# A decay attention with a softplus feed-forward on one core: the first score tile with 128 stationary columns, the magnitudes' sums listed later, the decay's parts on GpSimd, a shorter warm-up

## The chip, the cores and the metric

The kernel runs on one core of one Trainium2 chip. The metric is the device time of one execution in microseconds (us), the median of three runs. The engines are called as in the profile: PE is TensorE (PEld its weight loads), DVE VectorE, ACT ScalarE, POOL GpSimd, and SP issues nearly all DMAs (its queue is SPq in the rows).

## The reference

Eight batches of eight heads with 576 tokens and 64 features a head go through causal attention with a decay; its output, as 4608 rows of 512, goes through a feed-forward of 2048 with a softplus.

```python
scores = scale * np.matmul(q, k.transpose(0, 1, 3, 2))
cum = np.cumsum(np.log(np.clip(f, 0.0001, 1.0)), axis=-1)
decay = cum[:, :, :, None] - cum[:, :, None, :]
scores = np.where(causal, -1000000000.0, scores + decay)
attn = np.exp(scores - np.max(scores, axis=-1, keepdims=True))
attn = attn / (np.sum(attn, axis=-1, keepdims=True) + 1e-09)
x = np.matmul(attn, v)              # then (4608, 512)
h = x @ w_in
out = (np.maximum(h, 0.0) + np.log1p(np.exp(-np.abs(h)))) @ w_out
```

## The kernel before

The work is written as a list of small operations, and a planner in the kernel (`Plan`) turns the list into the five engines' programs. Each operation has an engine or a choice of engines, a cost, the operations that it needs and the buffers that it takes. The planner takes the operation that can start first by its costs, the one listed earlier when two are equal, appends it to its engine's program, and goes on. The result is a fixed order for each engine; on the chip an engine runs its program in that order and waits where an input is not there yet. A cost that differs from the chip's durations therefore makes no error in the result, only a wait.

**Jobs.** Attention is cut into jobs. Jobs 0 to 13 do batch 0 in float32, jobs 14 to 21 do batch 1 (their scores in float32, called mixed), and from job 22 on each job is one head of batches 2 to 7, 48 jobs, with float16 parts: q and k are each split into a high and a low float16 plane in a tile `T`. A job has five tiles of query rows: tile 0 has 64 rows, tiles 1 to 4 have 128. `stat_tile` lists the scores of a tile as two products into one PSUM bank (L1231 and L1233), then DVE's row minimum (L1238) and ACT's exponential (L1273), which frees the bank. Four banks serve the scores and other attention products. In the profile `s<-T` is a score product; the form `128*64 128x64 f16` means 128 contraction rows, 64 stationary columns and 64 moving columns. After the scores come the transposes or transposing DMAs, and the products with v (L1477, L1561).

**Feed-forward.** Blocks of 128 to 512 tokens run between the attention's operations: `h` products (L1676 in float32 for the first blocks, L1695 in float16), the softplus on ACT and DVE, and `acc` products (L1797, L1778).

**Magnitudes' sums.** Before a batch's float16 parts can be made, `size` finds how large v, q and k are. For each pair of heads of the batch eight jobs ahead it loads v (tile `vp`, L822) and q and k (tile `stage`, L836, two DMAs of 288 KB), and ACT sums the magnitudes (L829 and L840). `spread_tops` turns the sums into scales. A load's cost to the planner is an estimate from its size; the sum that needs it is placed where that estimate ends.

**Decay's parts.** `decay_parts` writes the cumulated decay of all 64 heads as three float16 rows (`eighth`, on ACT or DVE), with two subtractions on DVE between them (`remain`, L572 and L574), and stores them with two DMAs (L577). They are listed with job 13 and are needed from job 22 on.

**Start.** `warm` (L1969) puts three float32 products of 448 columns at the head of PE's program. While the planner's PE idles for over 0.5 us before the first `acc` product, `fill_gap` adds products without use (`fill`, L1984).

Of the kernel before, what the change touches and what calls it, by code (L numbers as in the profile page):

```python
# [30 lines left out]
SPARE_BIAS = 0.5  # L31
# [1 line left out]
WINDOW = 700  # L33
RATE = 262
PLAIN = 0
WARM = 3
CROSS = 2.2
FFN_RANK = 0
SHORT = 512
LARGE = 16.7  # L40
DELAY = 2
VALUES = 2.3

W_FROM, W_EACH = 0, 3
# [16 lines left out]
class Plan:  # L61
# [32 lines left out]
    def give(self, tag, ops, back=None):  # L94

        left = [len(ops), 0.0, back]
        for op in ops:
            self.gives.setdefault(op, []).append((tag, left))
# [105 lines left out]
def on_act(n, more=0.0, psum=False):  # L204
    return On("ACT", (0.067 if psum else 0.095) + n / 1200 + more)


def on_dve(n, fast=False, port=False, bias=0.0):
    return On("DVE", 0.071 + n / (1920 if fast else 960), bias, fast or port)
# [22 lines left out]
NO_ENGINE = On("", 0.0)  # L232
# [41 lines left out]
def tile_decay_attention_softplus_ffn(  # L274
# [18 lines left out]
    B, D, H, _, S = qkT.shape  # L293
    NT, DM = out.shape
    DFF = w_in.shape[1]
    P = 128
# [23 lines left out]
    add, give = plan.add, plan.give  # L320

    def add_dma(emit, kb, n=1, eng="SP", **more):
        return add(on_dma(kb, n, eng), emit, lag=dma_lag(kb, n, eng), **more)
# [20 lines left out]
    def back(box, key):  # L344
        return lambda: box[key, "back"]()
# [19 lines left out]
    MW = 448  # L365
# [133 lines left out]
    def decay():  # L499
        box = {}  # L500

        def load(e):
            box["f"] = buf("raw", [P, S], "fs")[0:BH]
            e.dma_start(out=box["f"], in_=f)

        def clip(e):
            e.tensor_scalar(box["f"], box["f"], 1e-4, 1.0, ALU.max, ALU.min)

        def log(e):
            e.activation(box["f"], box["f"], AF.Ln)  # L510

        def begin(e):
            cum["x"] = buf("x32", [P, NCC, S], "cum")[0:BH]
            cum[0] = cum["x"][:, 1, :]

        def eights(e, t, value):
            e.memset(cum["x"][:, t, :], value)

        def scan(e, a, z):
            c, x = cum[0], box["f"][:, a:z]  # L520
            e.tensor_tensor_scan(c[:, a:z], x, x, c[:, a - 1 : a] if a else 0.0, ALU.add, ALU.min)

        def split(e):
            ch, cl = box["hl"] = [buf("raw", [P, S], f"ch{x}", F32R)[0:BH] for x in "hl"]
            e.tensor_copy(ch, cum[0])
            e.tensor_sub(cl, cum[0], ch.bitcast(F32))

        def twice(ap):
            return bass.AP(ap.tensor, ap.offset, [ap.ap[0], [0, 2], ap.ap[1]])

        def store(e, r):
            x = aug_d[:, r, 0, :]
            to = bass.AP(x.tensor, x.offset, [x.ap[0], [5 * S, 2], x.ap[1]])
            e.dma_start(out=to, in_=twice(box["hl"][r].bitcast(F32)))

        def constant(e, r):
            e.dma_start(out=aug_d[:, 2 * r : 2 * r + 2, 1 - r, :], in_=twice(cum["x"][:, 2 - 2 * r, :]))

        f_ = add(NO_ENGINE, begin, takes=("x32",), lag=0.0)
        set_ = [  # L540
            add(on_fill(S), lambda e, x=x: eights(e, *x), after=[f_]) for x in ((2, 8.0), (0, -8.0))
        ]
        o = add_dma(load, BH * S / 256, takes=("raw",))
        o = add(on_dve(S, True), clip, after=[o])
        l = add(on_act(S), log, after=[o])
        decay_ready["eights"] = set_
        c = l
        for x, a, z in (("quad", 0, P), ("first", P, 2 * P), ("sums", 2 * P, S)):
            on = On("DVE", 0.11 + (z - a) / 480)
            c = decay_ready[x] = add(on, lambda e, a=a, z=z: scan(e, a, z), after=[c])  # L550
        give("raw", [c])
        def rest(after):
            s = add(On("DVE", 1.05, 0.0, True), split, after=[c, *after], takes=("raw", "raw"), loose=True)
            w = [add_dma(lambda e, r=r: store(e, r), BH * S / 128, after=[s] + first_rows) for r in range(2)]
            k = [add_dma(lambda e, r=r: constant(e, r), BH * S / 128, after=set_ + first_rows) for r in range(2)]
            for x in w:
                give("raw", [x])
            decay_ready["rows"] = add(NO_ENGINE, mark, after=w + k, lag=0.0)
            cum_used.extend([s] + k)

        def parts():
            def eighth(e, i):
                if i == 0:
                    box["rest"] = buf("raw", [P, S], "rest")[0:BH]
                    times(e, rows16[0:BH, 0], cum[0], 8.0)
                else:
                    copy(e, rows16[0:BH, i], box["rest"])

            def remain(e, i):
                x, of = box["rest"], rows16[0:BH, i]  # L570
                if i == 0:
                    e.scalar_tensor_tensor(x, cum[0], 8.0, of, ALU.mult, ALU.subtract)  # L572
                else:
                    e.tensor_sub(x, x, of)  # L574

            def store_parts(e, t):
                e.dma_start(out=aug16[:, SR - SR * t : 2 * SR - SR * t, t], in_=rows16[0:BH])  # L577

            o = [c]
            for i in range(SR):  # L580
                on = [on_act(S), on_dve(S, True, bias=SPARE_BIAS)]
                o = [add(on, lambda e, i=i: eighth(e, i), after=o, takes=() if i else ("raw",))]
                if i < SR - 1:
                    o = [add(subs(S), lambda e, i=i: remain(e, i), after=o)]
                if i == 0:
                    cum_used.extend(o)
            give("raw", o)
            decay_ready["parts"] = [add_dma(lambda e, t=t: store_parts(e, t), 216, after=o) for t in range(2)]

        return rest, parts  # L590
# [225 lines left out]
    def size(b, h):  # L816

        box = {}

        def load(e):  # L820
            box["v"] = buf("vpk", [P, 2, NCH * D], f"vp{b}_{h}")
            e.dma_start(  # L822
                out=box["v"].rearrange("p h (c d) -> p h c d", c=NCH),
                in_=vR[b, h - 1 : h + 1].rearrange("h p c d -> p h c d"),
            )

        def norm(e):
            x, at = box["v"].rearrange("p h c -> p (h c)"), h // 2
            e.activation(x, x, AF.Abs, scale=2.0**-16, accum_out=sizes[b % 2][:, at : at + 1])  # L829

        qk = stage[:, NBL * P : NBL * P + 2 * S]

        def load_qk(e):
            for i in range(2):
                to = qk[64 * i : 64 * i + 64].rearrange("p (h s) -> p h s", h=2)
                e.dma_start(out=to, in_=qkT[b, :, h - 1 : h + 1, 1 - i])  # L836

        def norm_qk(e):
            at = H // 2 + h // 2
            e.activation(qk, qk, AF.Abs, scale=2.0**-16, accum_out=sizes[b % 2][:, at : at + 1])  # L840

        if h % 2 == 0:
            return
        ld = add_dma(load, 320, takes=("vpk",))
        r = [add(on_act(2 * NCH * D, 0.19), norm, after=[ld] + size_read.get(b - 2, []))]
        give("vpk", r)
        if b > 1:
            ld = add_dma(load_qk, 576, 2, takes=("qkp",))
            r.append(add(on_act(2 * S, 0.19), norm_qk, after=[ld] + size_read.get(b - 2, [])))
            give("qkp", r[1:])  # L850
        size_ops.setdefault(b, []).extend(r)
        if h == H - 1:
            (spread_sizes if b < 2 else spread_tops)(b)
# [150 lines left out]
    def attention(job):  # L1004
# [200 lines left out]
        def stat_tile(ti):  # L1205
# [12 lines left out]
            for i, (a, z, acc) in enumerate(pieces):  # L1218
# [3 lines left out]
                def scores(e, box=box, a=a, z=z):  # L1222
                    o = keep_bank(box, "bank", "att", f"s{n}_{ti}_{a}")[:, 0 : z - a]
                    box["o"] = o[0:n_q]
                    if plain:
                        e.matmul(  # L1226
                            o, part32(0, q0, q0 + P), part32(1, a, z), start=True, stop=not quad,
                        )
                        return
                    o = box["o"]  # L1230
                    e.matmul(o, qA[:, q0:end], kA[:, a:z], start=True, stop=False)  # L1231
                    r = ST if mixed_ else S16
                    e.matmul(o, qB[0:r, q0:end], kB[0:r, a:z], start=False, stop=True)  # L1233

                def row_min(e, box=box, w=z - a, i=i, final=final):
                    right = MW - P + n_q if final else w
# [730 lines left out]
    warming = {}  # L1967

    def warm(e):  # L1969

        o = keep_bank(warming, "o", "h", "warm")
        for _ in range(WARM):
            e.matmul(o[:, 0:MW], cmask[:, 0:P], cmask, start=True, stop=True)

    give("h", [add(On("PE", 1.3 * WARM), warm, takes=("h",), after=mask_set)], back(warming, "o"))

    filling = []

# [9 lines left out]
    for n in range(len(jobs) + 1):  # L1988
# [26 lines left out]
            units.append(cur["fin"])  # L2015
        if n == nplain:
            plan.slack = SLACK
        if n == nstart - 1:
            decay_parts()
        if n == nfirst:  # L2020
            decay_rest(wrote[0][0][2:])
# [74 lines left out]
```

## Time and profile before

| | |
|---|---|
| median of three runs | 1037.95 us (1036.82 to 1038.4) |
| the profiled execution: its own time | 1036.13 us |
| its span, first to last instruction | 1034.4 us |
| PE busy | 1015.8 us of the span |
| DVE and ACT busy | 816.3 and 812.7 us |
| POOL busy | 87.6 us |
| mean granted TensorE clock | 0.997 |

The span and the profiled execution's own time differ by 1.7 us, which lies before the first and behind the last instruction. That execution is 1.8 us below the median of the three runs. Matmuls are pipelined, so PE's busy time says that it had something in flight, not that it ran at its peak; how far apart two products start tells more.

### The profile page before, as it was taken

What the parts mean: (1) busy time and instruction counts of PE and PEld (TensorE: products, weight loads), DVE (VectorE), ACT (ScalarE), POOL (GpSimd) and SP (SyncE); (2) the same over time, 40 slices, a digit from 0 to 9 for tenths busy, and PEclk for the clock granted to TensorE, in tenths of its full rate; (3) what the DMA queues carried; (4) which work ended last, traced back from release to release, by engine and by line L of the source; (5) the groups of instructions that cost most, each with busy time, mean ns of one, the idle gap of its engine ahead of it and who ended that gap; (6) DMA issues with size and microseconds to landing.
All of it is one profiled execution on the core that took longest, in us unless ns stands there. A gap on an engine that the chain in (4) does not pass through costs nothing.

```text
span 1034.4 us, 19420 instructions
## 1 busy us (share of the span) xinstructions
PE 1015.8 (98%) x6545; PEld 596.8 (58%) x6545; DVE 816.3 (79%) x2287; ACT 812.7 (79%) x1948; POOL 87.6 (8%) x182
## 2 busy tenths in 40 slices
PE   8999999989999999999999999999999999999998
PEld 6767777757655544456655544456655544456554
DVE  7789999879978997798879988898778988652332
ACT  7789899879879888888878997788768887654554
POOL 3233100100010000100010000100010000000000
PEclk9999999989999999999999999999999999999999
DMA  9968765656876586696666677556635564410000
GB/s 238 277 216 267 184 174 128 158 147 153 199 175 157 147 191 162 138 200 170 160 155 155 171 194 154 126 127 158 151 93 120 128 154 106 76 47 24 22 1 30
DMA packets 250931, 150.83 MB, mean 146 GB/s; under 512 B 194496, under 2 KB 225728, under 8 KB 250832
## 3 DMA queue, kind: packets, MB, share of 16 engines
q1 hardware_dynamic: 250664, 149.45, 58.4%
q8 instruction: 51, 0.84, 0.3%
q14 instruction: 48, 0.39, 0.1%
q10 hardware_dynamic: 168, 0.15, 0.0%
HBM read 72.00 MB, written 11.39 MB: 81 GB/s over the span
## 4 chain that ended last, share of the span: by engine, by line
PE 81%; ACT 6%; DVE 6%; DMA 4%; issue 2%; SPq 1%; POOL 0%; DVEq 0%; ACTq 0%; POOLq 0%
PE h L1695 30%; PE acc L1778 28%; PE o L1561 4%; PE s L1231 3%; PE s L1233 3%; PE acc L1797 3%; PE h L1676 2%; DMA stage<-in_qkT 2%; PE s L1226 2%; ACT p L1273 2%; PE o L1477 1%; PE b L1421 1%; DVE s L1238 1%; ACT stage L840 1%; DMA stage<-cross 1%
## 5 line engine op out<-in xcount | busy, mean ns | idle before, releaser
L1778 PE MATMUL acc<-wo,gh 128*128 128x512 f16 x1632 | 381.8, 379 | 0.3 <-ACT gh L264 0.2
L1695 PE MATMUL h<-xh,wi 128*128 128x256 f16 (+2 forms) x1536 | 372.0, 318 | 1.9 <-ACT p L1273 0.9
L1695 PEld LDWEIGHTS <-wi 128*128 128x128 f16 x2304 | 221.7, 98 | 133.1 <-issue 6.3
L1778 PEld LDWEIGHTS <-gh 128*128 128x128 f16 x1632 | 157.2, 98 | 169.1 <-ACT gh L264 0.7
L1695 PE MATMUL h<-xl,wi 128*128 128x256 f16 (+2 forms) x768 | 231.9, 318 | 0.7 <-DVE xl L1650 0.7
L1273 ACT ACTIVATE p<-s,negm 128x288 f32<-128x288 f32 (+7 forms) x384 | 183.0, 480 | 39.9 <-DVE negm L1238 34.8
L1741 DVE SCALAR_TENSOR_TENSOR e<-e,x 128x512 f32<-128x512 f32 (+1 forms) x152 | 95.3, 627 | 82.1 <-ACT e L1729 81.7
L1726 ACT ACTIVATE e<-h,h_down 128x512 f32<-128x512 f32 (+1 forms) x152 | 96.8, 637 | 74.8 <-PE h L1695 74.5
L1238 DVE CUSTOM_DVE_ANT_0 s<-s,cmask,s_down 64x64 f32<-64x64 f32 (+4 forms) x240 | 114.8, 490 | 32.0 <-PE s L1233 28.2
L1752 DVE SCALAR_TENSOR_TENSOR gh<-e,g_up,gh 128x512 f16<-128x512 f32 (+1 forms) x152 | 104.5, 688 | 24.4 <-ACT gh L264 23.9
L264 ACT ACTIVATE gh<-e,g_up 128x512 f16<-128x512 f32 (+1 forms) x116 | 77.9, 672 | 37.2 <-DVE e L1741 36.0
L1231 PE MATMUL s<-T 128*64 128x64 f16 (+1 forms) x336 | 96.6, 299 | 5.0 <-ACT p L1273 4.0
L1733 ACT ACTIVATE x<-h,h_down 128x512 f32<-128x512 f32 (+1 forms) x152 | 96.7, 636 | 0.1
L1729 ACT ACTIVATE e<-e 128x512 f32<-128x512 f32 (+1 forms) x160 | 93.7, 586 | 0.0
L1233 PE MATMUL s<-T 70*64 70x64 f16 (+1 forms) x336 | 92.5, 282 | 0.1
L1273 ACT ACTIVATION_READ_ACCUMULATOR p<-s,negm 128x1 f32 (+1 forms) x384 | 75.9, 198 | 0.0
L1345 DVE SCALAR_TENSOR_TENSOR stage<-p,rsum,stage 64x64 f16<-64x64 f32 (+3 forms) x144 | 70.7, 517 | 0.1
L1345 DVE SCALAR_TENSOR_TENSOR cross<-p,rsum,cross 64x64 f16<-64x64 f32 (+3 forms) x144 | 70.4, 518 | 0.0
L1289 POOL TENSOR_TENSOR lsum<-lsum,part 128x5 f32<-128x5 f32 x48 | 16.0, 333 | 575.3 <-ACT p L1273 575.3
L1561 PE MATMUL o<-stage,v 128*64 128x64 f16 (+4 forms) x408 | 53.2, 284 | 0.0
L1561 PE MATMUL o<-cross,v 128*64 128x64 f16 (+4 forms) x408 | 53.2, 284 | 0.0
L1238 DVE DVE_READ_ACCUMULATOR2_ANT negm<- 128x1 f32 (+1 forms) x384 | 52.9, 138 | 0.0
(183 smaller groups left out, 1289.0 us busy)
## 6 DMA issues: line engine op xcount, KB each, us to landing
raw<-in_qkT SPq DMA_DIRECT2D x112, 144.0 KB
stage<-in_qkT SPq DMA_DIRECT2D x48, 288.0 KB
vr<-in_vR SPq DMA_DIRECT2D x64, 160.0 KB
T<-T SPq DMA_DIRECT2D x64, 144.0 KB
vp<-in_vR SPq DMA_DIRECT2D x28, 320.0 KB
out<-ob SPq DMA_DIRECT2D x35, 256.0 KB
stage<-in_w_in SPq DMA_DIRECT2D x16, 512.0 KB
stage<-in_w_out SPq DMA_DIRECT2D x16, 512.0 KB
```

Of the source, the lines that this page charges most:

```text
L1231: e.matmul(o, qA[:, q0:end], kA[:, a:z], start=True, stop=False)
L1233: e.matmul(o, qB[0:r, q0:end], kB[0:r, a:z], start=False, stop=True)
L1238: e.tensor_tensor_reduce(out=box["o"], in0=box["o"], in1=cmask[0:n_q, right - w : right], scale=by, scalar=m0 if i else 3.0e38, op0=ALU.ad ...
L1273: e.activation(o, box["o"], AF.Exp, bias=m1, scale=-1.0, accum_out=acc)
L1345: e.scalar_tensor_tensor(to2, of, f_, to1, ALU.mult, ALU.subtract)
L1561: e.matmul(o[r : r + D, w - m : w], s["v16"][:, c, D * y : D * y + D], turned(s["pT"], c, x, m), start=i == 0, stop=i == len(ms) - 1, tile ...
L1695: e.matmul(o, l, r, start=m == 0, stop=m == 11)
L1726: e.activation(box["e"], st["h", u][:, 0:gw], AF.Exp, scale=h_down[:, si, g])
L1733: e.activation(box["x"], st["h", u][:, 0:gw], AF.Copy, scale=h_down[:, si, g])
L1741: e.scalar_tensor_tensor(o, box["e"], LARGE, x, ALU.min, ALU.max)
L1752: e.scalar_tensor_tensor(box["l"], box["e"], up, box["h"], ALU.mult, ALU.subtract)
L1778: e.matmul(st["acc", tt], l, r[fc], start=first and m == 0, stop=last and m == 2,)
```

## The change

It has four parts. In the float16 jobs the scores of tile 0 take 128 stationary columns where they took 64: the bank's tile keeps 128 rows, of which 64 are used as before. After each of the magnitudes' loads a mark without an engine is added, whose follower the planner places 5 us later (`LATE`). The three float16 rows of the decay go to POOL alone, and the parts are listed with job 10 (`nstart - PARTS`) and no longer with job 13. The third warm-up product has 192 columns where it had 448, and the planner is told so.

```diff
-WARM = 3
+WARM = 448, 448, 192
+PARTS = 4
+LATE = 5.0
@@ in parts()
-                on = [on_act(S), on_dve(S, True, bias=SPARE_BIAS)]
+                on = On("POOL", 0.2 + S * 0.0026)
@@ in size()
         ld = add_dma(load, 320, takes=("vpk",))
+        ld = add(NO_ENGINE, mark, after=[ld], lag=LATE)
...
             ld = add_dma(load_qk, 576, 2, takes=("qkp",))
+            ld = add(NO_ENGINE, mark, after=[ld], lag=LATE)
@@ in scores()
-                    o = box["o"]
-                    e.matmul(o, qA[:, q0:end], kA[:, a:z], start=True, stop=False)
+                    if mixed_:
+                        o = box["o"]
+                    last = q0 + o.shape[0]
+                    e.matmul(o, qA[:, q0:last], kA[:, a:z], start=True, stop=False)
                     r = ST if mixed_ else S16
-                    e.matmul(o, qB[0:r, q0:end], kB[0:r, a:z], start=False, stop=True)
+                    e.matmul(o, qB[0:r, q0:last], kB[0:r, a:z], start=False, stop=True)
@@ in warm()
-        for _ in range(WARM):
-            e.matmul(o[:, 0:MW], cmask[:, 0:P], cmask, start=True, stop=True)
+        for w in WARM:
+            e.matmul(o[:, 0:w], cmask[:, 0:P], cmask[:, 0:w], start=True, stop=True)
@@
-        if n == nstart - 1:
+        if n == nstart - PARTS:
             decay_parts()
```

The order changes on all engines, since the planner's choices follow each other. Three places are shown. First PE's program at tile 0 of job 24, before and then after; a name such as `s24_0_0` is job 24, tile 0, first key column 0, and the size at the end is that of the output.

```order
L1695 MATMUL h3_3_2918<-xh3_1785,wi16_7_1401 128x256
L1231 LDWEIGHTS T16_0_2467
L1231 MATMUL s24_0_0_2936<-T16_0_2467 64x64
L1233 LDWEIGHTS T16_0_2467
L1233 MATMUL s24_0_0_2936<-T16_0_2467 64x64
L1695 LDWEIGHTS wi16_4_990
```

```order
L1701 MATMUL h3_3_2919<-xh3_1718,wi16_7_1164 128x256
L1237 LDWEIGHTS T16_0_2478
L1237 MATMUL s24_0_0_2937<-T16_0_2478 128x64
L1239 LDWEIGHTS T16_0_2478
L1239 MATMUL s24_0_0_2937<-T16_0_2478 128x64
L1701 LDWEIGHTS wi16_4_1001
```

The products stand at the same place; their output has 128 rows where it had 64. Of the 48 such tiles, 3 follow a product with 64 stationary columns (L1561) before; of the new order 5 do (behind L1567 and L1483, the same lines there).

Next ACT's program around the exponentials of job 22, before. L840 is the sum of `stage`, L829 that of `vp`; `p..<-s22_3_0` is the exponential of tile 3.

```order
L1273 ACTIVATE p0_512_94,lsum2_81<-s22_3_0_2685,negm2_77 128x448
L270 COPY cross_102<-b21_2_2718 128x448
L829 ACTIVATE vp4_1_2693,size0_125<-vp4_1_2693 128x640
L270 COPY cross_102<-b21_3_2734 128x512
L840 ACTIVATE stage_103,size0_125<-stage_103 128x1152
L1273 ACTIVATE p0_640_95,part2_85<-s22_4_0_2690,negm2_77 128x288
L1273 ACTIVATE p0_640_95,lsum2_81<-s22_4_288_2740,negm2_77 128x288
L270 COPY x32_1_1679<-o21_2753 64x384
L1273 ACTIVATE p1_68_96,lsum3_82<-s23_0_0_2744,negm3_78 64x64
```

After:

```order
L1279 ACTIVATE p0_512_94,lsum2_81<-s22_3_0_2678,negm2_77 128x448
L272 COPY cross_102<-b21_2_2707 128x448
L272 COPY cross_102<-b21_3_2715 128x512
L266 ACTIVATE T16_0_2478<-raw24_2361,qk1_0_135 128x576
L1279 ACTIVATE p0_640_95,part2_85<-s22_4_0_2688,negm2_77 128x288
L1279 ACTIVATE p0_640_95,lsum2_81<-s22_4_288_2721,negm2_77 128x288
L831 ACTIVATE vp3_5_2631,size1_126<-vp3_5_2631 128x640
```

No sum stands between tiles 3 and 4 of job 22 any more. The pair of sums that stood there (`vp4_1`, batch 4) now stands in jobs 26 and 27, and the last sum of batch 3 in job 25 where it was in job 22; batch 3's scales are taken at job 28 in both orders.

Last POOL's program at the start of the kernel: the conversions of the weights (L671 before, L673 after), before and then after.

```order
L671 TENSOR_SCALAR wol2_dt_float32_401<-stage_103 128x512
L270 COPY cross_102<-rsum0_87 128x128
L671 TENSOR_SCALAR wol3_dt_float32_462<-stage_103 128x512
L671 TENSOR_SCALAR wol4_dt_float32_503<-stage_103 128x512
L671 TENSOR_SCALAR woh5_dt_float32_531<-stage_103 128x512
L671 TENSOR_SCALAR woh6_dt_float32_597<-stage_103 128x512
```

```order
L673 TENSOR_SCALAR wol3_dt_float32_435<-stage_103 128x512
L272 COPY cross_102<-rsum0_87 128x128
L268 TENSOR_SCALAR rows16_122<-cum_150 64x576
L673 TENSOR_SCALAR wol4_dt_float32_498<-stage_103 128x512
L272 COPY cross_102<-rsum1_88 128x128
L272 CAST rows16_122<-rest_485 64x576
L673 TENSOR_SCALAR woh5_dt_float32_549<-stage_103 128x512
L272 CAST rows16_122<-rest_485 64x576
L673 TENSOR_SCALAR woh6_dt_float32_600<-stage_103 128x512
```

The three rows of the decay (`rows16`) stand among the conversions of the weights, between the conversions of `wol3` and `woh6`. The new order also has 16 `fill` products before the first `acc` product, in five groups; before there were 8 in two groups.

## Rows read from the trace of the kernel before

**Rows 1.** Stages: us, busy time by engine, PE's granted clock, DMA share, GB/s.

```profile
20.00:40.00 20.00, 19.30 (x140) 14.92 (x140) 18.54 (x60) 17.83 (x50) 5.83 (x7) 1.00 1.01 247
500.00:550.00 50.00, 50.00 (x335) 28.10 (x333) 39.82 (x119) 37.78 (x92) 4.73 (x8) 1.00 0.56 138
220.00:230.00 10.00, 5.51 (x40) 3.47 (x39) 5.30 (x15) 5.91 (x17) 0.39 (x2) 0.80 0.56 140
230.00:240.00 10.00, 10.00 (x80) 8.37 (x79) 9.77 (x23) 9.06 (x21) 0.75 (x2) 0.86 0.41 94
```

**Rows 2.** PE in order of time at three places: start us, duration us, instruction.

```profile
324.72 1.67 PE L1778 MATMUL acc<-wo,gh 128*128 128x512 f16 x7
326.33 0.22 PE L1231 MATMUL s<-T 128*64 128x64 f16 x1
326.38 0.20 PE L1233 MATMUL s<-T 70*64 70x64 f16 x1
326.51 0.34 PE L1695 MATMUL h<-xh,wi 128*128 128x384 f16 x1
...
395.39 0.19 PE L1231 MATMUL s<-T 128*64 128x64 f16 x1
395.55 0.39 PE L1695 MATMUL h<-xh,wi 128*128 128x512 f16 x1
...
260.36 0.25 PE L1231 MATMUL s<-T 128*128 128x192 f16 x1
260.53 0.30 PE L1231 MATMUL s<-T 128*128 128x320 f16 x1
```

**Rows 3.** PE in order of time, 227 to 230 us; in brackets idle time and releaser.

```profile
227.14 0.53 PE L1231 MATMUL s<-T 128*128 128x448 f16 x1 [3.56 <-ACT p L1273]
228.77 0.37 PE L1695 MATMUL h<-xh,wi 128*128 128x256 f16 x1 [0.24 <-DVE xh L266]
229.82 0.37 PE L1695 MATMUL h<-xl,wi 128*128 128x256 f16 x1 [0.68 <-DVE xl L1650]
```

**Rows 4.** ACT in order of time at that place, and the issue of the DMA.

```profile
225.35 1.16 ACT L840 ACTIVATE stage<-stage 128x1152 f32<-128x1152 f32 x1 [3.35 <-DMA stage<-in_qkT]
...
218.45 1.33 SPq L836 DMA_DIRECT2D stage<-in_qkT  x2
```

**Rows 5.** ACT's waits by what ended them: us in total, times, longest.

```profile
ACT stage L840 <- DMA stage<-in_qkT: 12.9, 8, 3.4
```

**Rows 6.** ACT and PE in order of time around 400 us.

```profile
398.86 1.16 ACT L840 ACTIVATE stage<-stage 128x1152 f32<-128x1152 f32 x1 [2.70 <-DMA stage<-in_qkT]
...
400.45 0.35 PE L1231 MATMUL s<-T 128*128 128x448 f16 x1 [0.41 <-ACT p L1273]
401.60 0.38 PE L1695 MATMUL h<-xh,wi 128*128 128x512 f16 x1 [0.60 <-ACT x L1733]
```

**Rows 7.** PE at the start, in order of time.

```profile
2.34 4.85 PE L1973 MATMUL warm<-cmask 128*128 128x448 f32 x6 [2.34 <-POOL cmask L473]
7.12 0.69 PE L1226 MATMUL s<-T 64*128 64x128 f32 x2
7.65 0.38 PE L1246 MATMUL s<-eye8p,cum 64*128 64x128 f32 x2
7.87 0.38 PE L1247 MATMUL s<-cum,eye8m 64*128 64x128 f32 x2
```

**Rows 8.** The decay's rows: durations in ns (min/median/max), first and last start, forms.

```profile
L905 POOL TENSOR_SCALAR rows<-s_up x12: 1637/1637/2069, 197.6 to 772.9; 8x576 f16<-8x576 f32 x12
L270 ACT CAST rows<-rest x2: 663/667/671, 105.9 to 109.8; 64x576 f16<-64x576 f32 x2
L572 DVE SCALAR_TENSOR_TENSOR rest<-cum,rows x1: 854/854/854, 104.3 to 104.3; 64x576 f32<-64x576 f32 x1
```

**Rows 9.** POOL in order of time: the conversion of `woh6`.

```profile
41.88 0.78 POOL L671 TENSOR_SCALAR woh_dt_float<-stage 128x512 uint16<-128x512 uint16 x1 [6.92 <-DMA stage<-in_w_in]
```

**Rows 10.** PE's `fill` products: durations in ns, first and last start, form.

```profile
L1984 PE MATMUL fill<-cmask x16: 272/275/275, 19.9 to 24.1; 128*128 128x128 f32 x16
```

More of the change, by code (lines that the diff above doesn't have):

```diff
@@ L1971, in warm @@
         o = keep_bank(warming, "o", "h", "warm")
-        for _ in range(WARM):
-            e.matmul(o[:, 0:MW], cmask[:, 0:P], cmask, start=True, stop=True)
-    give("h", [add(On("PE", 1.3 * WARM), warm, takes=("h",), after=mask_set)], back(warming, "o"))
+        for w in WARM:
+            e.matmul(o[:, 0:w], cmask[:, 0:P], cmask[:, 0:w], start=True, stop=True)
+    give("h", [add(On("PE", 0.003 * sum(WARM)), warm, takes=("h",), after=mask_set)], back(warming, "o"))
     filling = []
```

## The prediction

> **What bounds the kernel now.** I read the stages first, then the order of time at the places that the change touches, then the waits. In the float16 jobs PE is never idle in the record: 50.00 of 50 us between 500 and 550 us, while DVE has 39.82 and ACT 37.78 [rows 1]. There the time is the distance at which PE starts its products, and DVE and ACT have some 10 us in 50 to spare, so a shorter distance is worth its full length. Two stretches are different. Between 20 and 40 us DVE is busy for 18.54 us and ACT for 17.83 of 20, and the DMA engines are full (1.01) [rows 1]: the start is paced by weights that arrive and by DVE. And between 220 and 230 us PE is busy for only 5.51 of 10 us, with a granted clock of 0.80, and of 0.86 in the next 10 us [rows 1]. That is the one place late in the kernel where PE stands still for long.
>
> A weighing of durations against distances is needed first. The record gives a 512-column product 379 ns of flight, but seven of them that start at 324.72 us and last 1.67 us start 0.215 us apart (1.67 less 0.38 of the last one's flight, over six). All prices below are distances between starts.
>
> **Tile 0.** Of the seven `acc` products the last one starts at 324.72 + 6 x 0.215 = 326.01 us. The two products of tile 0, 64 columns each, start at 326.33 and 326.38, and the next one at 326.51 [rows 2]. From the last `acc` product to the product behind the tile these are 0.50 us; 0.215 of it is the `acc` product's own, so the tile costs 0.285 us. For comparison, two products with 128 stationary and 192 moving columns start at 260.36 and what follows them at 260.53 [rows 2]: 0.17 us for three times the columns, 0.085 each. The difference must lie where 64 and 128 stationary columns meet: 0.10 us more before the first (0.32 for 0.215) and 0.13 behind the second. A third place confirms it: at 395.39 us the tile follows a product that also has 64 stationary columns, and then the two take 0.16 us together [rows 2], 0.12 us less than at 326 us. With 128 columns throughout, both meetings go. What is left is two products of 64 moving columns. The trace has no such product behind a load of 128, so I bound it: not over the 0.085 us of 192 columns, not under their share by columns, 0.085/3 = 0.03 us. I take 0.05, the distance of the two at 326 us, which is nearest in form. The tile then costs 0.10 in place of 0.275 (the mean of the two sides of the rounding at 0.285), 0.175 us less, with ends 0.105 and 0.22. Of the 48 tiles 43 gain it; in the new order five stand behind a product with 64 columns, where the meeting is only moved and nothing is won. The sum is 43 x 0.175 = 7.5 us, between 4.5 and 9.5.
>
> The Trainium skill, TensorE: Matmul & The Clock Gate, section Weight-path perf modes, says that weights load fast when there are 128 of them and they are not float32. That agrees with 0.285 against 0.17 us in this trace. The same page's section Back-to-back issue gap gives about 81 ns a product for a stream of weight load and 128-column matmul; by that figure, an estimate, two products would cost 0.16 and the tile would gain 0.12 us, or 5 us in all. It speaks against part of the gain; no run here shows that stream.
>
> **The sums, listed 5 us later.** At 225.35 us ACT starts the sum of `stage` after 3.35 us of waiting for its DMA, which was issued from 218.45 us on [rows 4]. ACT was therefore there at 222.00 us, 3.55 us after the issue began. Behind the sum in ACT's program stand the exponentials that free PSUM banks, and PE waits 3.56 us for one, then 0.24 and 0.68 us for the split of x, which ACT makes after that [rows 3]. PE's idle time here is 3.56 + 0.24 + 0.68 = 4.48 us. Then it runs slowly: 2 x (0.20 x 10 + 0.14 x 10) = 6.8 us at the lower level of 1.2 GHz instead of 2.4 [rows 1]. If that time is in one piece it begins at 226.0 us, in the idle stretch; 4.8 us of it are busy, and half of these, 2.4 us, are lost. With the mark ACT is due at the sum at least 5 us later after the issue, 8.5 us, and the data were there after 6.9 us. So this wait goes; and the new order has no sum there at all. What goes with it is ACT's 3.35 us and, if PE's remaining 1.1 us of idle time does not lower the clock, the 2.4 us: 5.8 us. Bounds: 3.35 us if the clock falls anyway, 6.9 us if PE's whole idle time goes.
>
> Seven other waits of this kind make up 12.9 - 3.4 = 9.5 us of ACT's time [rows 5], but PE mostly does not notice. At 398.86 us ACT has waited 2.70 us and PE then waits 0.41 and 0.60 us [rows 6]. I take 0.8 us for these, between 0 and 1.2. The sums' buffers come free 5 us later, so loads move; the last sum of batch 3 moves from job 22 to job 25, but its scales are first asked for at job 28, so no wait is added there.
>
> **The warm-up.** Six passes lie between 2.34 and 7.12 us, 0.80 us each, and the first scores follow directly [rows 7]. The third product's two passes shrink by 256 of 448 columns: 2 x 0.80 x 256/448 = 0.9 us. The warm-up ran at half speed (1.8 ns a column, against 0.86 for two passes of 128 columns in the 0.22 us from 7.65 to 7.87 [rows 7]). Scores that start 0.9 us earlier may run at that speed for as long, which returns half. Behind them weights and DVE set the pace. I take 0.3 us, between 0 and 0.9.
>
> **The decay's parts.** Three ACT operations of about 0.67 us leave the time around 105 us [rows 8], 2.0 us at most. On POOL the nearest operation, the same 576 columns from float32 to float16, takes 1.64 us [rows 8], so 4.9 us enter between the conversions of `wol3` and `woh6`. Before the conversion of `woh6` POOL waited 6.92 us for the DMA [rows 9], which covers it; without that cover the weights of a block would be up to 4.9 us late. The two subtractions on DVE, one 0.85 us [rows 8] and one like it, move to a stretch where DVE has 1.5 us free in 20: up to 1.7 us lost. The two stores move with them into a time of full DMA engines. Gain 2.0 and loss 1.7 are the ends; I take nothing.
>
> **Reordering.** The planner now puts in eight more `fill` products. Their two passes take 0.22 us, like those at 7.65; with PE idle they cost nothing, otherwise 8 x 0.22 = 1.8 us. Those of before run between 19.9 and 24.1 us [rows 10]; whether the added ones fall into idle time no row can show, so I take half, 0.9 us.
>
> **Sum.** -7.5 - 5.8 - 0.8 - 0.3 + 0.9 = -13.5 us. From the profiled execution's own 1036.13 us (span 1034.4) this gives 1022.6; that execution was 1.8 us under the median of the runs, 1037.95, and from the median it is 1024.4 us.
>
> **The rivals.**
> - *The wait moves.* All orders are new, and some other DMA, say a `vp` or `raw` load at the change from float32 to float16 jobs, lets ACT wait and PE with it; the clock falls once more. For it: eight such waits are in the profile, and SP's order has changed around them. Against: the mark gives every sum 5 us. Then nothing of the 5.8 and 0.8 us is won: 1037.95 - 7.5 - 0.3 + 0.9 = 1031.
> - *The weight loads bound tile 0.* The two products cost 0.17 us as at 192 columns. 43 x 0.105 = 4.5 us, and the time is 1027.4 us. For it: 0.085 us is the shortest distance in the trace behind a float16 load of 128 columns. Against it: that is also what 192 moving columns need, and two small products start 0.05 us apart at 326 us [rows 2]. The 81 ns of the Trainium skill's page TensorE: Matmul & The Clock Gate, section Back-to-back issue gap, are close to this rival.
> - *Slower, or no change: DVE overfull at the start.* The subtractions come to DVE, which is busy for 18.54 of 20 us, and the decay's rows stand ahead of weights on POOL. If scores or the first blocks then come late, PE pauses as at 227 us, with the lower clock behind each pause. Such a pause cost 4.48 + 2.4 = 6.9 us. Two of them eat the gain (1038 us), and from the third on the kernel is slower (1045 us). For it: more `fill` products were planned, so the planner itself sees more pauses there. Against: POOL's cover of 6.92 us and a load of only 1.7 us on DVE.
>
> **How the numbers follow.** Forecast 0.52, the moved wait 0.18, the bound by loads 0.10, DVE overfull 0.20. A measurement of this kernel can tell about 0.2%, 2.1 us, from no change. The first three are faster, together 0.80; of the last 0.08 lie within 0.2% and 0.12 above. The likeliest time is 1024.4 us. Its own range is 1018 to 1030, the terms' bounds not all at one end. The range to hold 8 in 10 takes in the three faster cases: at the low end 9.5 + 6.9 + 1.2 + 0.9 + 2.0 = 20.5 us less is 1017.5, at the high end the moved wait with all 1.8 us of `fill` and two more us of reordering is 1034.
>
> **What the profile after would show.** The two products of tile 0 with 128 stationary columns, at 0.05 us, and 0.10 us from the first to the product behind the second; right up to 0.17. No wait of ACT for a `stage` load over 1 us, PE busy for over 9 of 10 us around 225 us, and a granted clock of 1.00 there. The first scores at about 6.2 us. `rows16` on POOL at about 1.64 us, with no weight conversion waited for by PE. The forecast is wrong if PE's waits sum to more than in this trace, if the clock falls in the first 130 us, or if PE is idle in the float16 jobs for DVE or ACT.

## The result and the profile after

The changed kernel takes 1021.21 us (median of four runs, 1018.19 to 1025.27) against 1037.74 us of the kernel before in the same comparison (1036.82 to 1038.4). The ratio is 0.9844, with a 95% interval from 0.9805 to 0.9883: 16.2 us less (12.1 to 20.2). The forecast was 1024.4 us, in a range of 1017 to 1034. The profiled execution took 1019.46 us, its span is 1017.7 us and the mean granted clock 0.996. PE is busy for 1006.1 us of the span in place of 1015.8, so the 16.7 us of the span are 9.7 us of shorter work and 7.0 us less idle time. One execution of all that follow, 1033.47 us in the second run of the changed kernel, lies more than 1.5% above the fastest of its kernel and is left out of that run's ratio.

The stages of the changed kernel, with the columns of [rows 1]:

```profile
20.00:40.00 20.00, 19.59 (x138) 14.92 (x139) 18.32 (x59) 17.27 (x48) 10.66 (x13) 1.00 0.94 251
220.00:230.00 10.00, 8.19 (x60) 6.06 (x57) 9.52 (x24) 8.87 (x22) 0.00 (x0) 0.83 0.56 147
230.00:240.00 10.00, 10.00 (x80) 7.45 (x79) 9.18 (x24) 9.46 (x24) 0.65 (x2) 1.00 0.84 219
```

The stretch around 225 us, where PE was busy for 5.51 of 10 us [rows 1], has 8.19 now, at a clock of 0.83. The stop is not gone, it is shorter. PE in order of time there, and at the stop of 56 to 60 us:

```profile
222.58 0.28 PE L1701 MATMUL h<-xh,wi 128*128 128x256 f16 x1 [0.83 <-DVE xh L268]
223.84 0.27 PE L1701 MATMUL h<-xl,wi 128*128 128x256 f16 x1 [0.98 <-DVE xl L1656]
...
58.60 0.27 PE L616 MATMUL top<-ident,tops 128*1 128x128 f32 x1 [1.78 <-ACT p L1279]
```

PE's wait of 3.56 us for an exponential [rows 3] has become 0.83 and 0.98 us for the two halves of x, which DVE makes. In the trace's record of the clock, the kernel before runs at half speed from 226.0 us for 6.8 us; the changed one from 60.7 us for 3.4 us, behind the stop at 58.60, and from 224.5 us for 3.4 us. In both kernels that is 6.8 us at half speed in all.

ACT's waits for a DMA over 1 us in total; no row of `stage<-in_qkT` or `vp<-in_vR` is left, where `stage` alone had 12.9 us [rows 5]:

```profile
ACT v L266 <- DMA vr<-in_vR: 1.9, 3, 1.2
```

Tile 0 between `acc` and `h`, as at 324.72 us in [rows 2]:

```profile
317.31 2.11 PE L1784 MATMUL acc<-wo,gh 128*128 128x512 f16 x9
319.25 0.19 PE L1237 MATMUL s<-T 128*128 128x64 f16 x1
319.28 0.20 PE L1239 MATMUL s<-T 70*128 70x64 f16 x1
319.31 0.33 PE L1701 MATMUL h<-xh,wi 128*128 128x384 f16 x1
```

The nine `acc` products are (2.11 - 0.38)/8 = 0.216 us apart, so the last starts at 319.04 us and the tile 0.21 us behind it: nothing is stretched. The product behind the tile starts 0.06 us after the tile's first. By the starts in the whole trace, the medians of before were 0.093 us of stretch ahead (0.309 for 0.216 behind an `acc` product), 0.052 between the two and 0.128 behind: 0.273 us. Now they are 0, 0.029 and 0.034: 0.063 us.

PE at the start, where the first scores stood at 7.12 us [rows 7], and the decay's rows:

```profile
2.33 3.94 PE L1979 MATMUL warm<-cmask 128*128 128x448 f32 x6 [2.33 <-POOL cmask L475]
6.20 0.49 PE L1230 MATMUL s<-T 64*128 64x128 f32 x2
6.52 0.38 PE L1252 MATMUL s<-eye8p,cum 64*128 64x128 f32 x2
...
27.23 1.66 POOL L268 TENSOR_SCALAR rows<-cum 64x576 f16<-64x576 f32 x1
33.38 0.75 DVE L574 SCALAR_TENSOR_TENSOR rest<-cum,rows 64x576 f32<-64x576 f32 x1
34.19 1.06 POOL L272 CAST rows<-rest 64x576 f16<-64x576 f32 x1 [1.25 <-DVE rest L574]
36.90 0.74 DVE L576 TENSOR_TENSOR rest<-rest,rows 64x576 f32<-64x576 f32 x1
37.71 1.14 POOL L272 CAST rows<-rest 64x576 f16<-64x576 f32 x1 [1.60 <-DVE rest L576]
```

The rows are made between 27 and 39 us, where the kernel before made them from 103 to 110 us on ACT [rows 8], and no weight conversion appears among PE's waits. Their three operations take 1.66, 1.06 and 1.14 us on POOL, 3.9 us where the prediction had 4.9.

### The profile page after: what moved, and what is told of

The parts are those of the page before. It is cut to its first block, busy times and chain, and to the rows that moved or that the text cites. A ratio compares the mean times of both kernels' runs of the same rounds, so it can differ in the third digit from the quotient of the medians.

```text
span 1017.7 us, 19448 instructions
## 1 busy us (share of the span) xinstructions
PE 1006.1 (99%) x6561; PEld 599.8 (59%) x6561; DVE 815.7 (80%) x2291; ACT 809.4 (80%) x1937; POOL 97.8 (10%) x189
## 4 chain that ended last, share of the span: by engine, by line
PE 95%; DVE 2%; DMA 1%; ACT 1%; issue 0%; SPq 0%; POOL 0%; DVEq 0%; ACTq 0%; POOLq 0%
PE h L1701 35%; PE acc L1784 34%; PE o L1567 5%; PE s L1237 4%; PE s L1239 4%; PE acc L1803 3%; PE h L1682 3%; PE o L1483 2%; PE b L1427 2%; PE s L1230 2%; DMA stage<-in_w_in 1%; DMA T<-in_qkT 1%; PE b L1430 0%; DVE wol_dt_float L681 0%; ACT p L1279 0%
## 5 line engine op out<-in xcount | busy, mean ns | idle before, releaser
L266 ACT ACTIVATE gh<-e,g_up 128x512 f16<-128x512 f32 (+1 forms) x112 | 75.4, 673 | 37.6 <-DVE e L1747 36.6
L1237 PE MATMUL s<-T 128*128 128x64 f16 (+1 forms) x336 | 93.3, 293 | 0.0
L1239 PE MATMUL s<-T 70*128 70x64 f16 (+1 forms) x336 | 91.0, 281 | 0.0
L1351 DVE SCALAR_TENSOR_TENSOR cross<-p,rsum,cross 128x512 f16<-128x512 f32 (+2 forms) x144 | 70.3, 518 | 0.1
L1351 DVE SCALAR_TENSOR_TENSOR stage<-p,rsum,stage 128x512 f16<-128x512 f32 (+2 forms) x144 | 70.2, 517 | 0.0
L1567 PE MATMUL o<-stage,v 128*64 128x64 f16 (+4 forms) x408 | 53.2, 284 | 0.0
L1567 PE MATMUL o<-cross,v 128*64 128x64 f16 (+4 forms) x408 | 53.2, 284 | 0.0
```

Source lines behind the costliest of these rows:

```text
L1237: e.matmul(o, qA[:, q0:last], kA[:, a:z], start=True, stop=False)
L1239: e.matmul(o, qB[0:r, q0:last], kB[0:r, a:z], start=False, stop=True)
L1351: e.scalar_tensor_tensor(to2, of, f_, to1, ALU.mult, ALU.subtract)
L1567: e.matmul(o[r : r + D, w - m : w], s["v16"][:, c, D * y : D * y + D], turned(s["pT"], c, x, m), start=i == 0, stop=i == len(ms) - 1, tile ...
```

## The experiments

Each ratio is to the kernel before on the same chip; its medians were 1036.31, 1035.81 and 1036.61 us for the three groups of four kernels. Microseconds are the ratio's distance from 1 times that median.

**Tile 0 alone.** The kernel before with

```diff
-                    o = box["o"]
-                    e.matmul(o, qA[:, q0:end], kA[:, a:z], start=True, stop=False)
+                    if mixed_:
+                        o = box["o"]
+                    last = q0 + o.shape[0]
+                    e.matmul(o, qA[:, q0:last], kA[:, a:z], start=True, stop=False)
```

and the second product likewise. 

> The kernel before with the first part of the change alone: the float16 scores of tile 0 with 128 stationary columns. The order of all five engines is that of before, only the 96 products differ. The forecast's term: 7.5 us less (4.5 to 9.5), so 1030.4 us. By the trace of the changed kernel, where the product behind the tile starts 0.063 us after the tile's first and the one ahead of it is no longer stretched, 0.21 us for each of 44 tiles: 9.2 us less, so 1028.7. Rival 'loads bound the tile': 4.5 us less, 1033.4. Rival 'the whole gain came with the new order': under 2 us less.

Measured: 1027.29 us, 0.9918 (0.9902 to 0.9935), 8.5 us less (6.7 to 10.2). The distances are those of the changed kernel, 0.028 and 0.034 us with no stretch ahead. With the order untouched, the gain is the tile's own; the bound by loads (4.5 us) lies outside.

**96 columns.** Which of two rules makes 64 columns dear?

```diff
-                    if mixed_:
-                        o = box["o"]
+                    o = box["o"] if mixed_ else o[0 : max(96, n_q)]
```

> The kernel before with 96 stationary columns in the float16 scores of tile 0 (64 of the 96 output rows are used), order as before. Theory A, the forecast's reading of the Trainium skill, page TensorE: Matmul & The Clock Gate, section Weight-path perf modes: loads are fast only at 128 columns, so 96 cost at least what 64 cost; the product ahead stays stretched by 0.09 us and the product behind the tile comes 0.13 us after the second; no gain, 1036 to 1040 us. Theory B, the Trainium skill, page TensorEngine Tiling (Array Packing), section Tiling Modes: a change between tiling modes drains the engine; 64 columns are a half of the array and 96 are none, so both meetings go as with 128: the product ahead is not stretched, and 8 to 9.5 us are won, 1028.5 to 1030 us.

Measured: 1029.11 us, 0.9937 (0.9916 to 0.9958), 6.5 us less (4.4 to 8.7). In order of time:

```profile
322.45 2.10 PE L1779 MATMUL acc<-wo,gh 128*128 128x512 f16 x9
324.39 0.19 PE L1232 MATMUL s<-T 128*96 128x64 f16 x1
324.42 0.21 PE L1234 MATMUL s<-T 70*96 70x64 f16 x1
324.46 0.33 PE L1696 MATMUL h<-xh,wi 128*128 128x384 f16 x1
```

The last `acc` product starts at 322.45 + 8 x 0.215 = 324.17, the tile 0.22 us later: no stretch. Over all tiles the product behind comes 0.045 us after the second, with 128 columns 0.034. So 96 columns cost 0.011 us more than 128, and nearly all of what 64 columns cost lies at the two meetings of half the array with the whole: 0.093 us ahead, and behind 0.094 against 128 columns (0.128 less 0.034) or 0.083 against 96. One more place shows the meeting: where the tile stands behind an `o` product with 64 stationary and 512 moving columns, the start of the tile comes 0.216 us after that product in the kernel before, and 0.312 us with 96 columns and 0.315 with 128. There the meeting is only moved, as the prediction said. The distances are those of theory B, though the median of the time falls short of its 8 to 9.5 us, which the interval reaches into: the Trainium skill, TensorEngine Tiling (Array Packing), section Tiling Modes, says that changing the tiling mode drains TensorE. This case's trace agrees, and the price here is the 0.093 and 0.094 us.

**The later sums alone.**

```diff
         ld = add_dma(load, 320, takes=("vpk",))
+        ld = add(NO_ENGINE, mark, after=[ld], lag=LATE)
```

and the same behind `load_qk`. 

> The kernel before with the second part alone: the magnitudes' sums planned 5 us behind the loads. The forecast's terms: 5.8 + 0.8 = 6.6 us less (3.35 to 8.1), 1031.3 us; no wait of ACT for a stage load over 1 us, and the clock does not fall around 225 us. Rival 'the wait moves': PE stops elsewhere near the first float16 jobs and the clock falls there; within 2 us of the kernel before. The changed kernel's trace speaks for a middle: the long wait went, but PE still stopped twice (0.83 and 0.98 us) and the clock fell for 3.4 us in place of 6.8; that would be 4 to 5 us less.

Measured: 1030.03 us, 0.9940 (0.9927 to 0.9952), 6.2 us less (5.0 to 7.6). The window at 220 us, and ACT's waits for DMAs:

```profile
220.00:230.00 10.00, 8.71 (x72) 6.29 (x71) 9.46 (x23) 8.87 (x25) 0.40 (x2) 1.00 0.38 89
```

```profile
ACT v L265 <- DMA vr<-in_vR: 2.7, 3, 1.3
ACT ti L659 <- DMA stage<-in_w_in: 0.9, 1, 0.9
ACT T L265 <- DMA vr<-in_vR: 0.2, 1, 0.2
```

No sum waits, and here the clock stays up at 220 us; it falls at 61.6 us for 3.4 us instead, where the kernel before had 6.8 us at half speed in all. The forecast's 6.6 us lie inside the interval.

**The decay's rows alone.**

```diff
-                on = [on_act(S), on_dve(S, True, bias=SPARE_BIAS)]
+                on = On("POOL", 0.2 + S * 0.0026)
...
-        if n == nstart - 1:
+        if n == nstart - PARTS:
```

> The kernel before with the third part alone: the decay's rows on GpSimd and three jobs earlier. The forecast's term: 0 (2.0 us less to 1.7 us more). Rival 'the start is disturbed': PE pauses before 130 us and the clock falls there, 5 us or more slower, since the changed kernel's clock fell at 60.7 us for 3.4 us. Rival 'GpSimd's rows free ACT at a place where PE waits': over 2 us faster.

Measured: 1032.36 us, 0.9965 (0.9949 to 0.9982), 3.6 us less (1.9 to 5.3). The forecast of nothing fails, and the clock does not fall before 130 us. The clock's record shows 6.8 us at half speed from 223.2 us, as long as in the kernel before.

**The warm-up alone.**

```diff
-        for _ in range(WARM):
-            e.matmul(o[:, 0:MW], cmask[:, 0:P], cmask, start=True, stop=True)
+        for w in WARM:
+            e.matmul(o[:, 0:w], cmask[:, 0:P], cmask[:, 0:w], start=True, stop=True)
```

with WARM = 448, 448, 192 and the planner's cost of the change. 

> The kernel before with the fourth part alone: warm-up products of 448, 448 and 192 columns; with it the planner puts in 16 fill products in place of 8. The forecast's terms: 0.3 us less (0 to 0.9) for the warm-up and 0.9 us more (0 to 1.8) for the fill products: 0.6 us more, within 0.3% of the kernel before. Rival 'the parts that gained apart (8.5, 6.2 and 3.6 us, together 18.3 where the whole change gave 16.2) are partly eaten by this part': 2 us or more slower than before, with PE's idle time or the clock's low time grown in the first 130 us.

Measured: 1.0004 (0.9969 to 1.0040), but the twelve executions are two groups, seven at 1029.92 to 1035.08 us and five at 1041.32 to 1044.86. All seven lie below the median of the kernel before, 1035.81 us, where the forecast had 0.6 us more; none of them was profiled, and why they gain stays open. The profiled one, of 1042.70 us, starts its pieces at 0.21 us a pass up to about 32 us, twice the distance of [rows 7].

**All but one part.** The changed kernel without the warm-up's part, without the decay's, and without the marks, each by taking the lines above back.

> The changed kernel with the old warm-up of three times 448 columns (8 fill products). By the forecast's terms 0.6 us less than the changed kernel, the same within the measurement. Rival 'this part costs 2 us': 1018 to 1019 us, ratio to before 0.982.

> The changed kernel with the decay's rows as before (ACT or DVE, listed with job 13). The forecast: no change (2.0 us more to 1.7 us less). If the 3.6 us that this part gave alone are its own, by work taken from ACT: 3 to 4 us slower than the changed kernel, ratio to before 0.988. If they came from the new order and shorter waits at places where the later sums also help: within 1.5 us of the changed kernel.

> The changed kernel with the sums planned at the end of the loads as before. The forecast's terms: 6.6 us slower than the changed kernel (3.35 to 8.1), ratio to before 0.991, with a wait of ACT for a stage load of 2 us or more near a place where PE stops. If parts overlap (decay's part alone also shortened PE's stops around 220 us): 2 to 4 us slower.

Measured: without the warm-up's part 1018.08 us, 0.9818 (0.9793 to 0.9842), 18.9 us less, five executions within 1.8 us. Without the marks 0.9885 (0.9858 to 0.9912), 11.9 us less; ACT waits for `stage` 7.2 us and for `vp` 6.4 us again. Without the decay's part 0.9894 (0.9856 to 0.9933), but that does not answer its question: three of six executions lie at 1030 us, and the profiled one of them runs its first 32 us at half speed as above; the other three lie at 1019.5 to 1024.9, within the changed kernel's 1017.5 to 1025.3. They show no loss of 3.6 us, but three executions are few.

**Tile 0 and the later sums together**, both diffs above. 

> The kernel before with the first two parts, tile 0 and the later sums: warm-up and decay's rows as before. The two alone gave 8.5 and 6.2 us; if they add, 14.7 us less, ratio 0.986, 1021 us. If decay's part has a gain of its own beside them (3.6 us alone), the kernel with all parts but the warm-up (1018.1 us, ratio 0.982) is 3 us or more faster than this one; if decay's part had only shortened the same stops, this one is within 1.5 us of it, 1018 to 1020 us.

Measured: 0.9880 (0.9852 to 0.9909), 12.4 us less; its interval and that of the kernel with the decay's part besides (0.9793 to 0.9842) do not meet. PE between 130 and 210 us in both, and in the kernel before (columns as in [rows 1]):

```profile
130.00:210.00 80.00, 77.38 (x586) 58.80 (x585) 72.50 (x219) 72.16 (x181) 8.90 (x9) 0.98 0.60 150
```

```profile
130.00:210.00 80.00, 79.44 (x603) 60.13 (x602) 75.04 (x228) 74.82 (x193) 11.55 (x11) 1.00 0.60 152
```

```profile
130.00:210.00 80.00, 78.32 (x595) 58.67 (x593) 73.32 (x230) 72.32 (x187) 7.97 (x7) 1.00 0.62 154
```

Without the decay's part PE is idle for 2.6 us (first fence) and 1.7 us (third), with it for 0.6 us (second). The same holds elsewhere: 2.2 us with the later sums alone and 1.5 with tile 0 alone; 0.3 with the decay's part alone and 0.0 in the changed kernel. The clock does not tell the first two apart: each has 3.4 us at half speed in all, from 144.1 us (the 0.98 above) and from 61.9 us.

**The warm-up's length with the order held.** The changed kernel once more; the changed kernel with `for w in (448, 448, 448):` in `warm` and the planner's cost left; and the kernel before with `for w in (448, 448, 192):` and its cost left.

> The changed kernel once more, for more executions. Theory 'the short warm-up sometimes does not raise the clock' (in two profiles of kernels with it the first pieces ran at 0.21 us a pass instead of 0.11 and the granted clock rose at 31.8 and 32.0 us instead of about 7): the four executions so far, 1018 to 1025 us, were all with the early rise; among more, some lie 8 to 10 us above the others, near 1028 to 1031 us. Rival 'those two profiles had another cause that the changed kernel does not share': all executions between 1017 and 1026 us.

> The changed kernel with the third warm-up product at 448 columns again, the planner's cost left as changed: the order of all engines is that of the changed kernel, only PE's warm-up lasts 0.9 us longer. Theory 'length decides the rise of the clock': no execution 8 us or more above the others, median at or under the changed kernel's, 1018 to 1022 us. Rival 'the new order with 16 fill products decides': the same two groups as in the changed kernel.

> The kernel before with the third warm-up product at 192 columns and nothing else; the order is that of before with 8 fill products. Theory 'length decides': two groups of executions, one at 1035 us or a little under (the forecast's 0 to 0.9 us less), one 8 to 10 us above it, and a spread as in warm_alone (1030 to 1045). Rival 'the new order with 16 fill products decides': one group at 1033 to 1038 us.

Measured: the changed kernel again 1021.41 us, 0.9865 (0.9824 to 0.9906), four executions at 1017.5 to 1021.9 and two at 1031.5 and 1033.5, the last of them the profiled one. With the long warm-up 1019.32 us, 0.9836 (0.9813 to 0.9858), all five at 1017.9 to 1020.3. The kernel before with the short one 1.0002 (0.9984 to 1.0020), eleven executions at 1034.0 to 1040.1 and one at 1042.8. PE's start in the changed kernel's execution of 1033.5 us:

```profile
2.32 4.00 PE L1979 MATMUL warm<-cmask 128*128 128x448 f32 x6 [2.32 <-POOL cmask L475]
6.25 0.79 PE L1230 MATMUL s<-T 64*128 64x128 f32 x2
6.84 0.63 PE L1252 MATMUL s<-eye8p,cum 64*128 64x128 f32 x2
...
31.51 1.08 PE L1990 MATMUL fill<-cmask 128*128 128x128 f32 x4
32.52 0.44 PE L1483 MATMUL o<-cross,vr 128*64 128x128 f32 x4
```

From 6.84 to the next pieces at 7.26 us two passes of 128 columns take 0.42 us, where the execution of 1019.46 us takes 0.23 from 6.52 to 6.75. PE works at 1.2 GHz until about 32 us: the first entry in the trace's record of the clock, a rise to full speed, stands at 32.3 us here and at 6.1 us in the other. The first mixed score starts at 133.8 us there and at 120.8 us in the other execution of the same kernel. With the long warm-up the rise is early, at 6.9 us:

```profile
2.32 4.79 PE L1979 MATMUL warm<-cmask 128*128 128x448 f32 x6 [2.32 <-POOL cmask L475]
7.05 0.48 PE L1230 MATMUL s<-T 64*128 64x128 f32 x2
7.37 0.38 PE L1252 MATMUL s<-eye8p,cum 64*128 64x128 f32 x2
```

## Why the prediction was right, step by step

**Tile 0** (7.5 us, 4.5 to 9.5). Right in mechanism and place: both meetings went. The size was a little low because the two products without a meeting take 0.063 us, not 0.10; 44 tiles (48 less three behind a product with 64 columns and the first, before which PE stands still) x 0.21 us = 9.2 us by the trace and 8.5 us by the run. What the prediction quoted for it, the fast load of 128 columns from the Trainium skill's page TensorE: Matmul & The Clock Gate (section Weight-path perf modes), was not the cause: 96 columns, which that rule leaves out, lose both meetings as well. The figure of about 81 ns from the same page of the Trainium skill (section Back-to-back issue gap) is for a load and a product of 128 moving columns; it is no floor for these two of 64 moving columns, 0.029 and 0.034 us.

**The sums** (5.8 + 0.8 us). The waits went as said, and alone the part gave 6.2 us. One clause failed: at 225 us PE was to be busy for over 9 of 10 us and the clock to stay up. In the changed kernel PE still stops there for 0.83 and 0.98 us, for x's halves on DVE, and the clock fell; with 6.8 us at half speed in all, the 2.4 us that the term had for the clock were not won in that execution. The prediction had read this stop wrongly: it put PE's last two waits of before, 0.24 and 0.68 us, down to ACT, while the rows name DVE [rows 3]. It is DVE's work that is left: a copy of x, the two halves and row minima between them, without a pause from 221.13 to 223.80 us. In the whole, the kernel without the marks is 4.3 us slower than the change (11.9 against 16.2 us).

**The decay's parts** (0; gain 2.0, loss 1.7). This step failed: alone the part gave 3.6 us. It counted the 2.0 us taken from ACT and charged the two DVE subtractions as a loss at the new place, but gave nothing for the 0.854 + 0.750 us that they leave behind on DVE at 104 and 109 us. The prediction looked at the place where the work arrives and not at the one from which it goes. With both ends the gain could have been 2.0 + 1.6 = 3.6 us; that the run gave just this number is not shown to be more than chance. Behind the old place PE was never idle, so nothing could be won there at once. The kernel before from 104 to 130 us, then the decay's part alone from 130 to 210 us:

```profile
104.00:130.00 26.00, 26.00 (x169) 18.32 (x167) 23.83 (x91) 21.69 (x51) 2.57 (x4) 1.00 0.70 182
```

```profile
130.00:210.00 80.00, 79.72 (x594) 59.70 (x594) 74.77 (x228) 73.24 (x187) 11.55 (x10) 1.00 0.64 162
```

With the part alone PE's idle time goes from 1.7 to 0.3 us between 130 and 210 us, from 5.1 to 3.7 us between 210 and 240, and from 1.9 to 0.9 us between 240 and 420: 3.8 of the 5.3 us between the two profiled spans (1034.4 and 1029.1). So most of the gain lies in shorter stops of PE; whether the freed engines or the new order shortened them stays open.

**The warm-up and the fill products** (0.3 less, 0.9 more). The first scores came at 6.20 us as said. What the prediction did not see is that the clock may then not rise for another 25 us. It weighed that scores that start 0.9 us earlier "may run at that speed for as long, which returns half"; in the execution above the delay is 13.0 us (133.8 less 120.8). Such a start was profiled in three kernels, all with the short warm-up and the 16 fill products. The long warm-up in the changed order gave none in five executions, the short one in the old order one candidate in twelve. So both may be needed; length alone is not shown to be the cause. Nor is it shown that the long warm-up excludes it: with 448 x 3, one execution of tile 0 and sums together lies at 1030.0 us (the others at 1021.9 to 1023.5), and two of 17 of the kernel before in the second group of kernels at 1041.8 and 1042.1 us, 6 us above their median, with the same mean of recorded clock (0.996) as its faster ones. None of these was profiled. The fill products, at 0.9 us, were not separated.

**The sum.** Tile 0, sums and decay alone add up to 8.5 + 6.2 + 3.6 = 18.3 us; the three together gave 18.9 (all but the warm-up). The whole change gave 16.2 and, the second time, 14.0. So the warm-up's part takes back some 2.7 to 4.9 us by the ratios, whose intervals overlap. The forecast's -13.5 came out near partly by luck: it missed a gain of 3.6 and a loss of about that size.

**The rivals.** *The wait moves* did not come as told, since no DMA holds ACT there; but the place still stops PE, for 1.81 in place of 4.48 us. *Loads bound tile 0* is refuted by the distances. *DVE overfull at the start* did not come: PE between 20 and 40 us is busy for 19.59 us in place of 19.30. Two signs named as proof of a wrong forecast did come. One is that PE waits in the float16 jobs, for DVE at 222 to 224 us and for ACT at 304 us (0.68 us). The other is the fall of the clock at 60.7 us; it costs half of 3.4 us, 1.7 us, and the stops there, 1.98 us, stand in place of three in the old order (0.40, 0.72 and 0.72 us) behind which the clock did not fall.

The fastest version run is the change without its warm-up part, 1018.08 us; the changed order with the long warm-up, 1019.32 us, is not told apart from it.

## What to carry to other kernels

Where a short float16 tile stands among full ones on PE, fill its stationary side up to the full width if rows may be thrown away: what it cost here is the meeting of two tiling modes, about 0.2 us for a pair of meetings, and not the load. When work is moved between engines or in time, price both ends, the place it leaves as well as the one it enters, and ask where PE stands still behind each. Before a warm-up is cut, take the spread of many executions, since here its benefit was lost in some executions only, and a median of four hid it.

## What the runs showed of the hardware that was not expected

The granted clock in the profile's rows did not show the late rise. Here is the window from 6 to 20 us of the changed kernel in the execution of 1033.5 us and in that of 1019.46 us, columns as in [rows 1]:

```profile
6.00:20.00 14.00, 14.00 (x60) 13.06 (x60) 4.88 (x28) 5.39 (x22) 1.62 (x4) 1.00 0.90 256
```

```profile
6.00:20.00 14.00, 13.84 (x104) 11.34 (x102) 11.05 (x49) 10.21 (x34) 3.77 (x6) 1.00 1.02 284
```

Both say 1.00, with 60 products in the one and 104 in the other. The column counts the time before the first entry of the record, 32.3 us in the one, as full speed; the distance between starts tells the level there.

The same stop does not always lower the clock. With the long warm-up and the same order PE stops at the same place around 222 us for as long, and the window reads

```profile
220.00:230.00 10.00, 8.21 (x76) 6.71 (x72) 9.80 (x24) 9.48 (x23) 0.00 (x0) 1.00 0.51 140
```

at 8.21 us busy, where the changed kernel had 8.19 us at 0.83: 76 products against 60 in 10 us. The same shows near 60 us: with the later sums alone PE stops for 2.43 us there and the clock falls at 61.6 us, and with tile 0 besides it stops for 2.58 us and the clock stays up.

Not every piece of half the columns paid the whole price. Tile 0 of the mixed jobs, 64 columns in float32, in the changed kernel:

```profile
120.27 0.72 PE L1682 MATMUL h<-x,woh_dt_float 128*128 128x128 f32 x5
120.75 0.27 PE L1237 MATMUL s<-T 128*64 128x64 f32 x1
120.86 0.22 PE L1239 MATMUL s<-T 68*64 68x64 f32 x1
120.92 1.14 PE L1682 MATMUL h<-x,woh_dt_float 128*128 128x128 f32 x8
```

The five `h` products are 0.11 us apart, so the last starts at 120.72 and the next of them at 120.92: 0.20 us, 0.09 more than between two of them. The eight from there last 1.14 us, where eight of them from 119.94 us on last 1.05, so another 0.08 us lies behind, and the tile costs some 0.17 us. Between float16 `h` products, at 144.85 us, it costs 0.10 us. The float16 tile cost 0.27 us before the change and 0.06 after it. Float32 as such does not spare a piece: in the kernel before, an `o` product of 64 columns in float32 starts 0.202 or 0.203 us behind a float16 `h` product at four places, where two such `h` products are 0.109 us apart. What makes the mixed tile cheaper was not tried.
